# A residual in bf16, GELUs in batches and another key order in a two-layer attention and mixer kernel

## The chip, the cores and the metric

The kernel runs on one core of one Trainium2 chip. The time is the device time of one execution in microseconds (us), as the median of several executions; there is one core, so the slowest core is that core. Five engines of the core appear in this text. PE multiplies matrices, ACT (ScalarE) computes exponentials, GELUs and scaled copies, DVE (VectorE) does elementwise work and statistics, POOL (GpSimd) does small work on the side, and SP only starts transfers here. Every run lists the mean clock that the throttle granted PE, as a share of full speed.

## The reference, cut to what matters

```python
B, S, D, H, F = 1, 2048, 448, 16, 1792          # Dh = 28

def _A_ref(x, wqkv, wo):                        # attention
    q, k, v = ...                               # x @ wqkv, 16 heads of 28
    scores = jnp.einsum("bhqd,bhkd->bhqk", q, k) * (Dh ** -0.5)
    p = _softmax(scores, axis=-1)
    return ... @ wo

def _B_ref(x, w1, w2, w3, w4):                  # mixer
    h = _gelu(_layernorm(x, axis=-1) @ w1)
    ...                                         # four quarters of h shifted along S, then @ w2
    x1 = x + hs
    h2 = _gelu(_layernorm(x1, axis=-1) @ w3) @ w4
    return x1 + h2

x = A_x                                         # everything is bf16
for _ in range(2):                              # written out in the original
    x = x + _A_ref(_layernorm(x), A_wqkv, A_wo)
    x = x + _B_ref(_layernorm(x), B_w1, B_w2, B_w3, B_w4)
```

The softmax needs 2 x 16 x 2048 x 2048 exponentials, about 134 million. GELU is needed on 2 x 2048 x (448 + 1792) elements. In the trace of the kernel before, a table load of 1.283 us stands wherever ACT changes from exponentials to its GELU function (9 times) or back (8 times). (Most of the 448-wide GELUs are built from a tanh, of which 32 stand in this trace, 28 with a mean of 642 ns and 4 with 410, none of them with a table load.)

## The kernel before: the parts that matter

The rows are cut into 16 tiles of 128. Four tiles make a unit of 512 queries (the last unit of layer 2 is halved). The program is written as many small generator tasks; a scheduler in the same file runs them against modelled durations, with a list of seeds (`MOVES`) that breaks its ties, and fixes one order of instructions for each engine before the kernel is built. The attention loop hands ACT one exponential after another. Each reads one to three PSUM banks of scores, and everything else has to fit around it.

```python
x_res = sb("x_res", [128, NT, D], FP32)          # the residual, 16 tiles
h2T   = sb("h2T", [128, 14, 512], BF16)          # w3's output, up to 4 tiles wide
...
# the exponential (t_attention)
yield op("act", e_dur(n), lambda e, ...: e.activation(out=PT[:, p0:p0 + cnt, :],
         in_=ps[:, b0:b0 + cnt, :], func=ACT.Exp, scale=SCALE), ..., tab="exp", main=n, ...)
...
# the second half of the mixer for up to four tiles (t_mixB)
yield from par(prio, [w3_group(fch) for fch in range(14)])   # PE -> PSUM -> DVE copy -> h2T
...
if not direct:
    yield op("act", c_act(14 * NW), lambda e: e.activation(out=h2T[:, :, hoff:hoff + NW],
             in_=h2T[:, :, hoff:hoff + NW], func=ACT.Gelu_apprx_tanh),
             reads=allk, writes=allk, tab="gelu", margin=1.0)     # one in-place GELU
...
yield from par(prio, [w4_tile(i, t) for i, t in enumerate(tiles)])
```

Nine such GELUs run, eight among the 821 exponentials and one right behind the last. In the trace each has a table load of 1.283 us ahead of it, and the eight have one behind them, ahead of the next exponential. The last three tiles of layer 2 use small GELUs that read PSUM directly ("direct"), after the exponentials.

The keys of a layer are worked through in parts, because a unit's queries can start before all keys exist. `ORDER` lists (unit, part) for the units that start that way:

```python
PARTS = {0: [(0, 4), (4, 8), (8, NT)], 1: [(0, 8), (8, 12), (12, NT)]}   # key tiles of a part
ORDER = {0: [(0, 0), (0, 1), (0, 2)], 1: [(0, 0), (1, 0), (0, 1), (1, 1), (0, 2), (1, 2)]}
```

Where the scheduler sees PE with too little work in the last 4 us, it inserts fillers: matmuls of ones into a free PSUM bank, whose result nobody reads. They are meant to keep PE's clock up; what taking 14 of them out of the head does is measured in e5_dip below (6.83 us at half clock).

```python
WIN, TARGET = 4.0, 0.8
def keep_pe_busy(self, until):
    ...
    while self.cur["pe"] + dur + 0.12 < until:
        used = ...                       # modelled busy time of PE in the last WIN us
        if used > self.TARGET * self.WIN:
            self.cur["pe"] = t + 0.1
            continue
        ...                              # pick a free bank
        self.P.add("pe", lambda e, b=pick: fn(e, b), reads, [key(pick)], t_end=t + dur)
```

## Time and profile before

The median is 1090.22 us of 3 runs (1089.98 to 1091.11). The profiled execution spans 1089.3 us.

| part of the span | us | how it is read |
|---|---|---|
| head, to the first exponential | 22.82 | timeline of ACT |
| first to last exponential | 1028.12 | windows; ACT busy 1014.31, idle 13.81 |
| tail, after the last exponential | 38.36 | windows |

The windows view of the kernel before gives that table. Its columns are the window, its length, then the busy time of PE, PEld (weight loads), DVE, ACT and POOL with the number of instructions, then the granted PE clock, the DMA share and GB/s. I cut the stretch of exponentials at 88.69 us, where ACT does a small scaling.

```profile
22.82:88.69 65.87, 62.33 (x487) 21.13 (x492) 58.48 (x160) 60.14 (x55) 6.17 (x8) 1.00 0.25 69
88.69:1050.94 962.25, 933.35 (x8519) 356.05 (x8529) 517.62 (x1139) 954.17 (x828) 41.66 (x49) 1.00 0.13 31
1050.94:1089.30 38.36, 34.03 (x332) 22.77 (x328) 18.73 (x48) 16.29 (x39) 5.03 (x7) 1.00 0.05 16
```

The reader is to see that ACT is idle 5.73 us in the first of these windows (65.87 - 60.14) and 8.08 us in the long one. PE looks just as busy, but its share contains fillers: 1225 of them in the whole program, 180.8 us. The bound is ACT: what takes work off ACT in the stretch shortens the run.

Where ACT's time goes is in its groups by shape (line, engine, operation, shapes, count, then busy us and the mean ns of one, then idle time before them), here those of the kernel before:

```profile
L1181 ACT ACTIVATE PT<-ps 128x1536 bf16<-128x1536 f32 x410 | 599.2, 1462 | 10.6 <-PE ps L1155 8.1
L1181 ACT ACTIVATE PT<-ps 128x1024 bf16<-128x1024 f32 x407 | 422.2, 1037 | 2.0 <-PE ps L1155 2.0
...
L1478 ACT ACT_TABLE_LOAD x9 | 11.5, 1283 | 0.2
L1181 ACT ACT_TABLE_LOAD x8 | 10.3, 1283 | 0.1
```

There are 18 table loads with the first one of the program: 9 for gelu, 8 back to exp. How one switch looks is in the timeline of ACT of the kernel before (start, duration, what):

```profile
600.17 1.28 ACT L1478 ACT_TABLE_LOAD   x1
601.46 3.19 ACT L1478 ACTIVATE h2T<-h2T 128x3584 bf16<-128x3584 bf16 x1
604.67 1.28 ACT L1181 ACT_TABLE_LOAD   x1
605.97 2.37 ACT L1181 ACTIVATE PT<-ps 128x1024 bf16<-128x1024 f32 x2
```

Each instruction starts where the one before it ended. A pair of loads costs 2 x 1.283 us here and nothing more that can be seen.

The start of the stretch, in the same view of the same kernel, has the longest single wait (in brackets: how long ACT was idle before, and what ended it):

```profile
22.82 7.14 ACT L1181 ACTIVATE PT<-ps 128x1536 bf16<-128x1536 f32 x6 [0.20 <-PE ps L1155]
34.90 29.52 ACT L1181 ACTIVATE PT<-ps 128x1536 bf16<-128x1536 f32 x26 [4.93 <-PE ps L1155]
```

### The profile page before, as it was taken

Reading aid. Unit: us, or ns where it says so; the run is one execution under the profiler, and the core shown is the slowest. Engines: PE = TensorE matmul, PEld = TensorE weight load, DVE = VectorE, ACT = ScalarE, POOL = GpSimd, SP = SyncE. Lnnn points to the kernel's source line nnn. Section 1 sums busy time; section 2 is a strip of 40 time slices with the busy share of each in tenths; the row PEclk is TensorE's granted clock in tenths of the full one; section 3 lists DMA queues with packets and bytes.
Section 4 is the critical chain, followed back from the end, with each engine's and each line's share of the span. In section 5 each row is a group of like instructions: output and inputs, shape, how many; then the busy total and the mean of one; then the engine's idle time right before and its main releaser. Section 6 shows DMA issues by size and latency. Waiting matters only on the chain.

```text
span 1089.3 us, 21738 instructions
## 1 busy us (share of the span) xinstructions
PE 1048.6 (96%) x9482; PEld 411.8 (38%) x9501; DVE 610.5 (56%) x1414; ACT 1044.3 (96%) x938; POOL 59.5 (5%) x80
## 2 busy tenths in 40 slices
PE   8999999999999999999999999999999999999998
PEld 4333333334333433333334333343333333434455
DVE  7985348411683358533787345525884646566453
ACT  6899999999999999999999999999999999999983
POOL 3100000000010000100001000000001000000010
PEclk9999999999999999999999999999999999999999
DMA  7222070000000000000011101222201000110000
GB/s 197 78 69 69 21 182 20 16 1 20 20 2 20 20 21 20 20 1 20 20 40 45 30 30 50 78 68 50 55 5 35 14 20 11 34 25 11 14 16 22
DMA packets 76968, 40.64 MB, mean 37 GB/s; under 512 B 61192, under 2 KB 70280, under 8 KB 76872
## 3 DMA queue, kind: packets, MB, share of 16 engines
q1 hardware_dynamic: 74760, 35.58, 13.0%
q0 software_dynamic: 2112, 3.67, 1.4%
q8 instruction: 74, 1.21, 0.5%
q14 instruction: 22, 0.18, 0.1%
HBM read 14.20 MB, written 8.13 MB: 21 GB/s over the span
## 4 chain that ended last, share of the span: by engine, by line
ACT 57%; PE 36%; DVE 5%; issue 1%; DMA 0%; SPq 0%; ACTq 0%; DVEq 0%
ACT PT L1181 50%; PE ps L639 10%; PE ps L1155 10%; PE ps L1205 8%; PE ps L642 4%; PE ps L1540 4%; ACT h2T L1478 4%; ACT gt L1297 1%; ACT L1478 1%; ACT L1181 1%; DMA h2T<-in_A_wqkv_dram 0%; DVE qT L909 0%; ACT h2T L1468 0%; DVE hT L1288 0%; DVE qT L944 0%
## 5 line engine op out<-in xcount | busy, mean ns | idle before, releaser
L1181 ACT ACTIVATE PT<-ps 128x1536 bf16<-128x1536 f32 (+1 forms) x821 | 938.8, 1247 | 12.6 <-PE ps L1155 10.1
L1155 PE MATMUL ps<-qT,kT 32*128 32x512 bf16 (+1 forms) x2304 | 319.4, 360 | 12.8 <-ACT PT L1181 7.1
L1205 PE MATMUL ps<-PT,vaug 128*32 128x512 bf16 (+1 forms) x2304 | 263.6, 362 | 3.0 <-ACT PT L1181 0.8
L1540 PE MATMUL ps<-ones_bf 128*128 128x256 bf16 x1225 | 180.8, 276 | 2.6 <-DVE hot L673 1.1
L1155 PEld LDWEIGHTS ps<-qT,kT 32*128 32x128 bf16 x2304 | 80.1, 91 | 260.7 <-ACT PT L1181 149.3
L1471 DVE CAST h2T<-ps 128x512 bf16<-128x512 f32 (+2 forms) x126 | 73.8, 586 | 126.1 <-PE ps L639 91.9
L1540 PEld LDWEIGHTS ps<-ones_bf 128*128 128x128 bf16 x1225 | 102.1, 98 | 81.2 <-issue 57.9
L639 PE MATMUL ps<-xT,w 112*128 112x512 bf16 (+6 forms) x581 | 118.1, 324 | 1.6 <-DVE h2T L1471 0.6
L1205 PEld LDWEIGHTS ps<-PT,vaug 128*32 128x32 bf16 x2304 | 67.6, 94 | 130.9 <-issue 76.3
L639 PE MATMUL ps<-w,h2T 128*128 128x448 bf16 x302 | 68.9, 354 | 5.3 <-ACT h2T L1478 5.0
L639 PEld LDWEIGHTS ps<-xT,w 112*128 112x128 bf16 (+1 forms) x581 | 45.7, 104 | 49.3 <-issue 26.0
L642 PE MATMUL ps<-xT,w 112*32 112x512 bf16 (+3 forms) x780 | 63.6, 340 | 0.3 <-DVE uin L1489 0.2
L1227 DVE SCALAR_TENSOR_TENSOR u_sb<-uin,fct,ps 128x512 f32<-128x512 f32 x24 | 17.8, 742 | 62.6 <-PE ps L1205 59.1
L642 PE MATMUL ps<-w,h2T 128*32 128x448 bf16 x584 | 46.4, 368 | 4.5 <-ACT h2T L1478 4.5
L1496 DVE TENSOR_TENSOR x_res<-x_res,ps 128x448 f32<-128x448 f32 x16 | 9.8, 619 | 71.2 <-PE ps L639 48.5
L1478 ACT ACTIVATE h2T<-h2T 128x7168 bf16<-128x7168 bf16 (+2 forms) x9 | 45.1, 5015 | 0.1
L1430 POOL TENSOR_TENSOR mst<-mst,neghalf 128x1 f32<-128x1 f32 x32 | 23.8, 747 | 297.7 <-DVE mst L1428 297.7
L639 PEld LDWEIGHTS ps<-w,h2T 128*128 128x128 bf16 x302 | 25.0, 97 | 35.1 <-issue 11.7
L909 DVE TENSOR_SCALAR qT<-ps,bcol 128x512 bf16<-128x512 f32 (+1 forms) x24 | 15.3, 653 | 40.7 <-PE ps L639 39.3
L802 DVE BATCH_NORM_STATS2 st<-x_res 128x6 f32<-128x448 f32 x60 | 36.9, 615 | 0.7
L1332 POOL TENSOR_TENSOR mst<-mst,neghalf 128x4 f32<-128x4 f32 (+2 forms) x10 | 9.1, 906 | 486.9 <-DVE mst L1331 273.7
L642 PEld LDWEIGHTS ps<-xT,w 112*32 112x32 bf16 (+1 forms) x780 | 24.0, 95 | 11.8 <-DVE hT L1288 0.6
(141 smaller groups left out, 908.0 us busy)
## 6 DMA issues: line engine op xcount, KB each, us to landing
uscr<-u_sb SPq DMA_DIRECT2D x24, 256.0 KB, 2.0
uin<-uscr SPq DMA_DIRECT2D x24, 256.0 KB, 2.8
x_res<-in_A_x_dram POOLq DMA_DIRECT2D x4, 896.0 KB, 7.4
w<-in_B_w_dram SPq DMA_DIRECT2D x2, 1568.0 KB, 13.8
out_dram<-uin SPq DMA_DIRECT2D x16, 112.0 KB, 1.7
h2T<-in_A_wqkv_dram SPq DMA_DIRECT2D x2, 392.0 KB, 5.6
w<-in_B_w_dram SPq DMA_DIRECT2D x2, 392.0 KB, 8.3
xT<-xn SPq DMA_TRANSPOSE x32, 3.7
```

The lines of the kernel that those rows point to most:

```text
L639: return e.matmul(out=dst(0, m), lhsT=lhs(0, m), rhs=rhs, start=start, stop=stop)
L642: return [e.matmul(out=dst(a, min(m, a + 32)), lhsT=lhs(a, min(m, a + 32)), rhs=rhs, start=start, stop=stop, tile_position=(0, a)) for a i ...
L802: yield op("dve", 0.55, lambda e: e.bn_stats(out=st6[:, t, :], in_=w4[:, t, :] if staged else x_res[:, t, :]), reads=[(("w4",), t // 2) if ...
L909: yield op("dve", 0.06 + c_ps(nw), lambda e, b=b: e.tensor_scalar(out=dst, in0=ps[:, bi(b), 0:nw], scalar1=bias, scalar2=None, op0=ALU.add ...
L1155: yield op("pe", 0.005 if ph == h else 0.012 + W / 2400.0, lambda e, bk=bk, r0=32 * j, g=g, kc=kc, q0=q0, W=W, c0=W * h: e.matmul(out=ps[: ...
L1181: yield op("act", e_dur(n), lambda e, b0=b0, p0=p0, cnt=cnt: e.activation(out=PT[:, p0:p0 + cnt, :], in_=ps[:, b0:b0 + cnt, :], func=ACT.E ...
L1205: yield op("pe", 0.004 + nt * 0.0133, lambda e, j=j, rhs=rhs, vs=vs, i=i: e.matmul(out=ps[32 * j:32 * j + 32, UBK, 0:128 * nt], lhsT=vaug[ ...
L1227: yield op("dve", 0.06 + c_ps(W), lambda e: e.scalar_tensor_tensor(out=u_sb[:, 0:W], in0=uin[:, :], scalar=fct[:, L, p, g:g + 1], in1=ps[: ...
L1430: yield op("pool", 0.57, lambda e, t=t: e.tensor_tensor(out=mst[:, t, R3:R3 + 1], in0=mst[:, t, V3E:V3E + 1], in1=neghalf[:, 0:1], op=ALU. ...
L1471: yield op("dve", c_ps(NW), lambda e, fch=fch, b=b: e.tensor_copy(out=h2T[:, fch, hoff:hoff + NW], in_=ps[:, bi(b), 0:NW]), reads=[("ps", ...
L1478: yield op("act", c_act(14 * NW), lambda e: e.activation(out=h2T[:, :, hoff:hoff + NW], in_=h2T[:, :, hoff:hoff + NW], func=ACT.Gelu_apprx ...
L1540: SC.fill = (0.13, lambda e, b: e.matmul(out=ps[:, bi(b), 0:256], lhsT=ones_bf[:, :], rhs=ones_bf[:, :].unsqueeze(1).to_broadcast([128, 2, ...
```

## The change

The intent has three parts. The residual is kept in bf16, as the reference rounds it anyway. The GELUs of neighbouring groups of tiles run one right after the other, so that a pair shares the two table loads; for that `h2T` becomes twice as wide. In layer 2, unit 0 gets all its keys before unit 1 gets its last two parts. Around these, the loads of x go to SP's queue without conversion, and the scheduler has new seeds. The diff, cut to its core:

```diff
-    ORDER = {..., 1: [(0, 0), (1, 0), (0, 1), (1, 1), (0, 2), (1, 2)]}
+    ORDER = {..., 1: [(0, 0), (1, 0), (0, 1), (0, 2), (1, 1), (1, 2)]}
-    TAILB = [[NT - 3], [NT - 2, NT - 1]]
+    MIXB = [      # (tiles, first slot of h2T, batch; None is direct), for each layer
+        [([0, 1, 2], 0, 0), ([3, 4, 5, 6], 4, 0), ([7, 8, 9, 10], 0, 1), ([11, 12], 4, 2), ([13, 14, 15], 0, 2)],
+        [([0, 1, 2], 4, 0), ([3, 4, 5, 6], 0, 0), ([7, 8, 9, 10], 4, 1), ([11, 12], 0, 1), ([13], 2, None), ([14, 15], 4, None)],
+    ]
-        x_res = sb("x_res", [128, NT, D], FP32)
+        x_res = sb("x_res", [128, NT, D], BF16)
-        h2T = sb("h2T", [128, 14, 512], BF16)
+        h2T = sb("h2T", [128, 14, 1024], BF16)
...      # x: chunk 0 straight to x_res (before: to a second place in bf16, which the first tiles read)
-            for c in (1, 2, 3, 0)[:NCH]:
-                yield op("pool", 0.8, ... e.dma_start(out=x_res[:, 4 * c:4 * c + 4, :], ...
+            for c in range(1, NCH):
+                yield op("sp", 0.1, ... e.dma_start(out=x_res[:, 4 * c:4 * c + 4, :], ...
...
-                yield op("act", c_act(14 * NW), ... func=ACT.Gelu_apprx_tanh), ..., tab="gelu", margin=1.0)
+                yield ("sig", ("w3", L, tiles[0]))
+                yield ("wait", ("gelu", L, tiles[0]))
...
+        def t_gelu(L, batch):
+            for (t, h0, n) in batch:
+                yield ("wait", ("w3", L, t))
+            for k, (t, h0, n) in enumerate(batch):
+                ...
+                yield op("act", c_act(14 * NW), ... func=ACT.Gelu_apprx_tanh),
+                         reads=allk, writes=allk, tab="gelu", margin=0.0 if k else 1.0, glue=k > 0)
+                yield ("sig", ("gelu", L, t))
...      # MOVES: new seeds; now a list of lists, with one attempt for each (there is one list)
```

The first two parts belong together. The bf16 residual frees 16 x 448 x 2 = 14336 bytes of a partition, and the wider `h2T` takes 14 x 512 x 2 = 14336. So the main worth of the bf16 residual is that it makes room for the batching.

## The prediction

> **What bounds it now.** ScalarE (ACT). By the windows view it is busy 1014.3 of the 1028.1 us between the first attention exponential (22.82 us, timeline) and the end of the last (1050.94). The groups show 821 exponentials, 938.8 us. PE's 96% is padded by 1225 filler matmuls (180.8 us); DVE has 576 us there. Outside lie a head of 22.8 us and a tail of 38.4 us, chains across engines. Of ACT's 13.8 us idle in the stretch, 4.93 us are one wait, before the seventh exponential, for PE's scores.
>
> **Batched GELUs.** Before, each of 9 in-place GELUs (3.19, 4.68 or 6.18 us) has its own table load, and 8 loads bring exp back: 18 loads with the first. The built order of the new kernel has 12. [...] the trace shows 1283 ns, and at 600.17 us exp to GELU to exp runs 1.28, 3.19, 1.28 us[...], so I count only the load, plus the 0.1 us by which neighbouring exponentials overlap (58 take 66.7 us, mean 1.247 alone). Six loads fewer: -8.3 us. Given back: the last 256-wide GELU stood after the last exponential and now stands before the last ten: +3.1 us. GELU work is the same otherwise.
>
> **Key order.** Layer 2's segments break groups of exponentials more often: 823, +0.2 us. Unit 0 finishes earlier, so mixer work spreads better; that saves part of about 5 us of small waits in 12 places: -1.5 us. Risk: layer 2 needs the third key chunk some 24 exponentials (28 us) after layer 1's last GELU batch, before about 53. I work out the chain from there (w4, residual, statistics, transposes, K projection) as about 17 us, so no stall above 2 us.
>
> **bf16 residual.** Normalizations reading x_res fall from 513 to about 400 ns (the group that reads bf16 already), 88 of them, 10 us of DVE. Statistics (613 against 615 ns by input type) and adds with a PSUM operand (618, 619) don't gain. [...] DVE is off the path outside head and tail: under 1 us. The converting loads and the second copy of chunk 0 go, but loads landed before DVE used them: nothing.
>
> **Head and tail.** All but one of the Q projections now stand before the first scores (16 matmuls more, about 4 us of PE, partly in gaps): first exponential 2 to 3 us later, the 4.93 us wait shorter; together +1. The tail stays a chain PE, DVE, POOL, ACT; leftover w4 matmuls (28 before, about 36 now, most ahead of the transposes, where fillers stood) and 4.5 us of load and GELU move off it: -1.5 us.
>
> **Sum.** -8.3 +3.1 +0.2 -1.5 +1 -1.5 = about -7 us: **1083.0 us**, 8 in 10 between 1076 and 1089. Chances: faster by over 2% 0.03, within 2% 0.96, slower 0.01.
>
> **Signs.** 12 table loads; ACT busy between first and last exponential about 1009 us; 823 exponentials at unchanged durations; normalizations near 400 ns; tail 36 to 38 us; first exponential at 25 to 26 us; the wait near the seventh under 4 us.
>
> **What would make it wrong.** ACT stalling for layer 2's third and fourth key chunks (after about 512 exponentials); small waits after the longer breaks (about 13 us of GELU in one piece), when w4 matmuls for seven tiles crowd PE; a tail that grows because leftover matmuls don't fit its gaps; a much better head.

The sum came to -8.3 +3.1 +0.2 -1.5 +1 -1.5 = -7.0 us. The -8.3 are six loads of 1.283 us and six times the 0.1 us of overlap, which the page before shows: 821 exponentials of 1.247 us are 1023.8 us one by one, and ACT is busy with them for 938.8 us, so each overlaps by 0.10 us.

## The result, and the profile after

| | runs | median us | range us | granted clock of the runs |
|---|---|---|---|---|
| before | 4 | 1090.66 | 1089.98 to 1091.36 | profiled one 0.998 |
| after | 4 | 1086.46 | 1085.44 to 1086.76 | 0.995, 0.995, 0.997, 0.995 |

The ratio is 0.996, with a 95% interval of 0.9943 to 0.9977: within 2%, and a little faster. A ratio in this text is the mean time of one kernel's fast runs over the mean of the other's in the same rounds, so it is not quite the ratio of the medians quoted beside it. The prediction of 1083.0 us was 3.5 us too low, and its range of 1076 to 1089 held.

The same windows for the kernel after, cut at the same small scaling, which is at 90.49 us here:

```profile
30.11:90.49 60.38, 57.54 (x429) 18.60 (x434) 50.95 (x141) 58.26 (x53) 2.10 (x2) 1.00 0.27 75
90.49:1048.12 957.63, 929.93 (x8449) 354.14 (x8457) 505.95 (x1138) 950.30 (x827) 40.97 (x49) 1.00 0.13 31
1048.12:1084.60 36.48, 32.91 (x348) 22.07 (x345) 18.85 (x48) 12.82 (x39) 3.99 (x7) 0.99 0.07 23
```

These lines and those of before add up to the whole difference. The span is ACT's busy time in the stretch, plus the head with the waits of the first window (start of the first exponential and ACT's idle time to the cut), plus the later waits, plus the tail:

| us | before | after | change | predicted |
|---|---|---|---|---|
| ACT busy, first to last exponential | 1014.31 | 1008.55 | -5.76 | -5.0 (-8.3 +3.1 +0.2) |
| head and first waits (22.82 + 5.73; 30.11 + 2.12) | 28.55 | 32.23 | +3.68 | +1 |
| later waits of ACT | 8.08 | 7.33 | -0.75 | -1.5 |
| tail | 38.36 | 36.48 | -1.88 | -1.5 |
| span | 1089.30 | 1084.59 | -4.71 | -7 |

The part that was meant to gain has gained. The groups of ACT by shape, kernel after:

```profile
L1183 ACT ACTIVATE PT<-ps 128x1536 bf16<-128x1536 f32 x410 | 599.8, 1463 | 3.9 <-PE ps L1157 2.3 <-PE ps L1207 0.3
L1183 ACT ACTIVATE PT<-ps 128x1024 bf16<-128x1024 f32 x405 | 420.9, 1039 | 3.8 <-PE ps L1157 2.9 <-PE ps L1207 0.8
...
L1511 ACT ACT_TABLE_LOAD x5 | 6.4, 1283 | 0.1
L1183 ACT ACT_TABLE_LOAD x5 | 6.4, 1283 | 0.1
...
L1352 ACT ACT_TABLE_LOAD x1 | 1.3, 1283 | 0.0
```

With the first load of the program that is 12 loads instead of 18, and the exponentials last as long as before. One batch in the timeline of ACT, kernel after, shows two GELUs (of 4.68 and 6.17 us) between one pair of loads:

```profile
352.05 1.28 ACT L1511 ACT_TABLE_LOAD   x1
353.34 10.75 ACT L1511 ACTIVATE h2T<-h2T 128x5376 bf16<-128x5376 bf16 x2
364.11 1.28 ACT L1183 ACT_TABLE_LOAD   x1
```

The start of the stretch, in the same view, has moved by 7.29 us, where 2 to 3 us had been expected:

```profile
30.11 2.37 ACT L1183 ACTIVATE PT<-ps 128x1536 bf16<-128x1536 f32 x2
32.82 3.78 ACT L1183 ACTIVATE PT<-ps 128x1536 bf16<-128x1536 f32 x3 [0.35 <-PE ps L1157]
37.78 7.80 ACT L1183 ACTIVATE PT<-ps 128x1024 bf16<-128x1024 f32 x7 [1.18 <-PE ps L1157]
```

The wait of 4.93 us has become one of 1.18 us, which pays for half of the delay. Where much of the rest went shows in two views of the head. First the windows of the kernel before, then those of the kernel after; the clock is the third number from the end:

```profile
15.00:18.00 3.00, 1.86 (x23) 1.06 (x23) 2.24 (x8) 0.77 (x2) 0.00 (x0) 1.00 1.56 381
18.00:21.00 3.00, 3.00 (x15) 0.95 (x13) 3.00 (x12) 2.00 (x3) 0.00 (x0) 1.00 0.85 201
```

```profile
12.00:15.00 3.00, 1.62 (x21) 1.10 (x22) 1.46 (x3) 1.76 (x3) 0.00 (x0) 1.00 0.20 69
15.00:18.00 3.00, 1.84 (x26) 1.16 (x25) 2.18 (x11) 0.69 (x1) 0.55 (x1) 0.63 0.03 8
18.00:21.00 3.00, 2.55 (x10) 0.87 (x8) 1.51 (x9) 0.60 (x1) 0.86 (x1) 0.50 0.00 0
```

Before, PE's clock is full through the head. After, it is half from 15.76 to 22.59 us by the trace's record of the clock. That lasts 6.83 us. Second, the timeline of PE, kernel before and then kernel after:

```profile
14.51 1.02 PE L639 MATMUL ps<-xT,wq_pad 112*128 112x512 bf16 x4
...
17.45 2.02 PE L639 MATMUL ps<-xT,wk_pad 112*128 112x512 bf16 x8
```

```profile
9.65 2.14 PE L1547 MATMUL ps<-ones_bf 128*128 128x256 bf16 x18
13.29 0.43 PE L852 MATMUL ps<-ident,xn 128*112 128x128 bf16 x4 [1.50 <-ACT xn L894]
...
16.94 1.91 PE L643 MATMUL ps<-xT,wq_pad 112*128 112x512 bf16 x4 [1.16 <-DVE sc L761]
...
20.41 2.97 PE L643 MATMUL ps<-xT,wk_pad 112*128 112x512 bf16 x8
```

The same four matmuls take 1.91 us instead of 1.02, and the same eight 2.97 instead of 2.02. Ahead of it PE ran dry: the scheduler put 18 fillers (line L1547) before a wait for ACT that lasted 1.50 us, and then came small transposes and matmuls with one column.

A similar thing happens near the end, in both of these profiled runs. After the last long GELUs the fillers stop too early, PE is idle until the GELU ends (2.21 us before, 2.29 us after), and for 3.41 us of the w4 matmuls behind it the clock is at 0.50 (from 1014.3 us before, from 1032.9 us after). The timeline of PE, before and then after:

```profile
1006.89 4.43 PE L1540 MATMUL ps<-ones_bf 128*128 128x256 bf16 x39
1013.53 4.51 PE L642 MATMUL ps<-w,h2T 128*32 128x448 bf16 x56 [2.21 <-ACT h2T L1478]
```

```profile
1025.36 4.54 PE L1547 MATMUL ps<-ones_bf 128*128 128x256 bf16 x40
1032.19 7.17 PE L643 MATMUL ps<-w,h2T 128*128 128x448 bf16 x28 [2.29 <-ACT h2T L1511]
```

Up to the end of the program the falls in the traces last 3.41, 6.83 or 10.24 us, which is one, two or three times 3.41 us, and the clock in them is 0.50. Their length varies between runs of one kernel (6.83 us in the head of this profile of the kernel after, 10.24 us in that of e0_after). In the three batches of experiments below, the kernel before ran 29 times. In 10 of those the mean clock is 1.0 and the mean time 1090.03 us; in 19 it is 0.998 and the mean time 1091.36 us. The kernel after ran 9 times in all, never with a full clock, with a mean of 1086.56 us.

The bf16 residual, finally, shows in the groups of DVE. Kernel before, then kernel after:

```profile
L871 DVE TENSOR_SCALAR xn<-x_res,mv,rstd 128x448 bf16<-128x448 f32 x56 | 25.7, 513 | 1.1 <-POOL rstd L1004 1.1
...
L1404 DVE TENSOR_SCALAR x1b<-x_res,mv,mst 128x448 f32<-128x448 f32 x32 | 15.6, 506 | 0.1
```

```profile
L873 DVE TENSOR_SCALAR xn<-x_res,mv,rstd 128x448 bf16<-128x448 bf16 x56 | 19.6, 402 | 3.3 <-POOL rstd L1006 3.3
...
L1406 DVE TENSOR_SCALAR x1b<-x_res,mv,mst 128x448 f32<-128x448 bf16 x32 | 15.3, 506 | 0.1
```

The normalization with a bf16 output falls from 513 to 402 ns when its input is bf16 too. In the one with an fp32 output nothing changes (506 and 506).

### The profile page after: what moved, and what is told of

It is laid out like the page before. It is cut to its first block, busy times and chain, and to the rows that moved or that the text cites. A ratio compares the mean times of both kernels' runs of the same rounds, so it can differ in the third digit from the quotient of the medians.

```text
span 1084.6 us, 21565 instructions
## 1 busy us (share of the span) xinstructions
PE 1046.1 (96%) x9390; PEld 409.4 (38%) x9408; DVE 597.5 (55%) x1410; ACT 1036.5 (96%) x938; POOL 54.1 (5%) x76
## 4 chain that ended last, share of the span: by engine, by line
ACT 60%; PE 34%; DVE 5%; DMA 1%; issue 0%; SPq 0%; DVEq 0%; ACTq 0%
ACT PT L1183 53%; PE ps L643 12%; PE ps L1157 8%; PE ps L1207 7%; ACT h2T L1511 4%; PE ps L646 4%; PE ps L1547 2%; ACT gt L1299 1%; DMA h2T<-in_A_wqkv_dram 1%; ACT L1511 1%; ACT L1183 0%; DVE kT L911 0%; DVE st L805 0%; DVE hT L1290 0%; DVE xn L873 0%
## 5 line engine op out<-in xcount | busy, mean ns | idle before, releaser
L1183 ACT ACTIVATE PT<-ps 128x1536 bf16<-128x1536 f32 (+1 forms) x823 | 938.3, 1246 | 7.7 <-PE ps L1157 5.2
L1207 PE MATMUL ps<-PT,vaug 128*32 128x512 bf16 (+1 forms) x2304 | 249.8, 362 | 3.3 <-ACT PT L1183 1.4
L1547 PE MATMUL ps<-ones_bf 128*128 128x256 bf16 x1234 | 185.1, 277 | 2.5 <-DVE hot L677 1.1
L1547 PEld LDWEIGHTS ps<-ones_bf 128*128 128x128 bf16 x1234 | 102.4, 98 | 85.5 <-issue 62.8
L643 PE MATMUL ps<-xT,w 112*128 112x512 bf16 (+6 forms) x632 | 127.8, 323 | 0.8 <-ACT h2T L1470 0.4
L643 PEld LDWEIGHTS ps<-xT,w 112*128 112x128 bf16 (+1 forms) x632 | 50.5, 104 | 52.6 <-issue 29.6
L643 PE MATMUL ps<-w,h2T 128*128 128x448 bf16 x259 | 62.2, 362 | 4.0 <-ACT h2T L1511 4.0
L646 PE MATMUL ps<-xT,w 112*32 112x512 bf16 (+3 forms) x576 | 48.8, 349 | 0.1
L1490 DVE TENSOR_TENSOR uin<-x_res,ps 128x448 bf16<-128x448 bf16 x16 | 9.8, 619 | 66.1 <-PE ps L643 49.8
L1497 DVE TENSOR_TENSOR x_res<-x_res,ps 128x448 bf16<-128x448 bf16 x16 | 9.9, 621 | 64.3 <-PE ps L646 35.3
L805 DVE BATCH_NORM_STATS2 st<-x_res 128x6 f32<-128x448 bf16 x64 | 39.1, 615 | 2.1 <-DMA x_res<-in_A_x_dram 1.3
L1223 DVE STREAM_TRANSPOSE u_sb<-ps 128x512 f32<-128x512 f32 (+1 forms) x24 | 15.0, 625 | 34.5 <-PE ps L1207 34.5
```

Of the source, the lines that this page charges most:

```text
L643: return e.matmul(out=dst(0, m), lhsT=lhs(0, m), rhs=rhs, start=start, stop=stop)
L646: return [e.matmul(out=dst(a, min(m, a + 32)), lhsT=lhs(a, min(m, a + 32)), rhs=rhs, start=start, stop=stop, tile_position=(0, a)) for a i ...
L805: yield op("dve", 0.55, lambda e: e.bn_stats(out=st6[:, t, :], in_=x_res[:, t, :]), reads=[("x", t)], writes=[("st6", t)])
L1183: yield op("act", e_dur(n), lambda e, b0=b0, p0=p0, cnt=cnt: e.activation(out=PT[:, p0:p0 + cnt, :], in_=ps[:, b0:b0 + cnt, :], func=ACT.E ...
L1207: yield op("pe", 0.004 + nt * 0.0133, lambda e, j=j, rhs=rhs, vs=vs, i=i: e.matmul(out=ps[32 * j:32 * j + 32, UBK, 0:128 * nt], lhsT=vaug[ ...
L1547: SC.fill = (0.13, lambda e, b: e.matmul(out=ps[:, bi(b), 0:256], lhsT=ones_bf[:, :], rhs=ones_bf[:, :].unsqueeze(1).to_broadcast([128, 2, ...
```

## The experiments

The theory is that the missing 3 us were lost to PE's clock: the new head leaves PE with too little work between 12 and 18 us (busy 1.62 and 1.84 of 3.00 us in the windows above), the clock halves, and the head is late by about 2 us. The late fall adds to it. The rivals are these. The x loads moved to SP's queue, beside the loads of the weights, so perhaps they delay ACT's preparation of the weights, and the low clock is only a bystander. Or the head is late because more Q projections stand before the first scores, whatever the clock. Or the batching gives part of its saving back.

There are twelve runs in three batches, each batch on one chip: the first four kernels on one (before there: 1090.88 us median, 11 runs), b1_late, e5_dip, e8_dense and e6_unbatch on a second (before: 1091.12 us, 9 runs), and the last four on a third (before: 1091.26 us, 9 runs). All results were correct. Most edits act on the finished order of instructions, just before it is emitted. `P.ops["pe"]` is PE's list, and this helper adds n fillers behind its instruction i:

```python
def more_fill(i, n, bank=None):
    pe, at = P.ops["pe"], P.ops["pe"][i]
    fn = at.fn if bank is None else lambda e: SC.fill[1](e, bank)
    extra = [_Op("pe", fn, False) for _ in range(n)]
    ...                                   # same position in the global list
    pe[i + 1:i + 1] = extra
```

### e0_after: the changed kernel again

No edit. What was expected:

> The changed kernel again, as the yardstick for the other runs on this chip. About 0.996 of before, 1086.5 us; granted clock 0.995; in the head the clock at half from about 15.8 to 22.6 us, first exponential near 30.1 us.

Measured: 1086.88 us (1086.06 to 1087.46, 5 runs), ratio 0.9963 (0.995 to 0.9976), the clock 0.995 in all five. The profiled run had the clock at half for 10.24 us in the head, and its first exponential came at 31.74 us. The result repeats in this batch, and the fall of the clock in the head with it. The fall was 3.41 us longer than expected, and the first exponential came 1.6 us later than expected.

### e1_fill: fillers where PE ran dry

```diff
+        more_fill(78, 12)            # 18 fillers become 30, up to the transposes at 13.3 us
```

> The changed kernel with 12 more filler matmuls just before PE's idle stretch that ends at 13.3 us. Theory (the head is late because this idle stretch lets the TensorE clock fall to half from 15.8 to 22.6 us): the clock stays 1.0 there, the first exponential starts at 27 to 28 us instead of 30.1, and the run is 1.5 to 2.5 us shorter than e0_after. Rivals (the early loads of x, or the order with more Q projections in front): the first exponential moves by less than 0.3 us, and so does the time.

Measured: 1085.95 us (1084.6 to 1087.71, 5 runs), ratio 0.9956 (0.9944 to 0.9968). The clocks are 0.998, 1.0, 0.998, 0.995 and 0.995. The profiled run (1084.66 us) had no fall in the head, and its first exponential came at 27.92 us, 2.19 us earlier than in the kernel after; the late fall was there. The timeline of PE of this kernel shows the filled gap and the four matmuls at their full speed again:

```profile
9.42 3.45 PE L1547 MATMUL ps<-ones_bf 128*128 128x256 bf16 x30
13.27 0.43 PE L852 MATMUL ps<-ident,xn 128*112 128x128 bf16 x4 [0.39 <-ACT xn L894]
...
16.75 1.03 PE L643 MATMUL ps<-xT,wq_pad 112*128 112x512 bf16 x4 [0.99 <-DVE csum L746]
```

Twelve matmuls that compute nothing made the head faster in this run, which speaks for the theory. But two of the five runs have a mean clock as low as the kernel after, so this one gap isn't the whole condition. The time alone, with its overlapping intervals, would not have told e1_fill from e0_after.

### e2_xlate: the x loads held back

```diff
+        for x in P.ops["sp"][5:8]:                       # x chunks 1 to 3
+            x.deps[P.ops["sp"][3].ekey] = P.ops["sp"][3] # wait for the Q weights
```

> The changed kernel with the three loads of x (chunks 1 to 3) held back on SP until the Q weights have landed, as they were in before, where they stood behind POOL's work. Rival R1 (these loads take bandwidth from the weights): the Q weights land near 6.9 us instead of 8.9, the last of the first transposes comes at 12.5 instead of 13.3, and 0.8 us is gained; if the shorter idle stretch also keeps the clock up, 2 to 3 us. Clock theory alone: the clock still falls and at most 0.8 us is gained. Order theory: nothing.

Measured: 1086.16 us (1082.71 to 1087.7, 6 runs), ratio 0.9954 (0.9942 to 0.9966). The issue of these loads moved from 3.39 to 8.96 us, yet ACT's wait for the Q weights ended at 8.97 us, where it had ended at 8.88 in the kernel after and at 9.32 in e0_after. The profiled run had a fall of 10.24 us in the head, as long as that of e0_after, and the first exponential at 31.52 us. So the transfers were not what held ACT up, and this rival falls. One of its six runs had a clock of 1.0, and that run took 1082.71 us; the other five had 0.994 to 0.997 and took 1085.92 to 1087.7. In these six runs of one kernel on one chip, the time follows the clock.

### e3_both: the two together, with fewer fillers

```diff
+        ...                          # the dependency of e2_xlate
+        more_fill(78, 8)
```

> Both edits, with 8 fillers. If clock and loads are both causes: 2.5 to 3.5 us shorter than e0_after, first exponential at 26 to 27.5 us. What then remains against 22.8 us in before is the order, about 4 us of matmuls and evictions of the Q and V projections that now stand in front.

Measured: 1086.19 us (1084.51 to 1087.0, 5 runs), ratio 0.9955 (0.9944 to 0.9967), clocks 0.995, 0.998, 0.998, 0.997, 0.998. The profiled run still had a fall of 6.83 us in the head and its first exponential at 29.79 us. This was a miss: eight fillers did not hold the clock in the profiled run, and the experiment tells nothing about a sum of two effects. PE's wait before the transposes had shrunk to 0.56 us here and the clock fell, while in the profile of e1_fill it was 0.39 us and the clock stayed; two profiles show no threshold.

### e5_dip: the opposite edit, on the kernel before

If thin work on PE is the cause, taking fillers out of the head of the kernel before has to bring the fall there, with its loads and its order of Q projections unchanged.

```diff
+        for a, b in ((88, 92), (69, 79)):                # 14 fillers
+            gone = P.ops["pe"][a:b]
+            P.ops["pe"][a:b] = []
```

> The kernel before with 14 fillers of its head taken out (around 10 to 13 us), so that PE idles there as it does in the changed kernel. Clock theory: in most runs the clock falls to half in the head, mean clock 0.995 to 0.997, first exponential at 25 us instead of 22.8, 2 to 3 us longer than before. Rival (idle PE in the head costs nothing): no change, these fillers compute nothing that is used.

Measured: 1092.52 us (1091.85 to 1095.74, 5 runs), ratio 1.002 (1.0007 to 1.0032), clocks 0.997, 0.996, 0.995, 0.992, 0.997. The windows of this kernel:

```profile
12.00:15.00 3.00, 1.48 (x11) 0.96 (x12) 1.95 (x7) 2.59 (x4) 0.00 (x0) 0.50 1.55 389
15.00:18.00 3.00, 3.00 (x17) 1.15 (x16) 0.81 (x5) 0.69 (x1) 0.58 (x1) 0.50 1.55 381
```

The clock is half for 6.83 us, the four Q matmuls take 1.87 us instead of 1.02, and the first exponential comes at 25.37 us instead of 22.82. PE had less to do and finished later. Not all of the 2.55 us are the clock's: ACT's first normalization already started at 8.15 us instead of 7.34, ahead of the fall at 11.57 us. From that normalization to the first exponential it takes 17.22 us here and 15.47 to 15.49 us in all four profiles of this order without a fall in the head (before, e4_bf16only, b1_late, b2_late). So about 1.7 us are the clock's. That settles it for this head: with 14 fillers less the clock fell to half for 6.83 us, and that delayed the first exponential by about 1.7 us.

### b1_late: a failed edit

This was meant to fill the late gap of the kernel before. The search for the place was wrong, and the 18 fillers went into a busy place, where a run of 4 fillers became one of 22.

```diff
+        more_fill(ends[-2], 18)      # not the gap it was meant for
```

> The kernel before with 18 more fillers in its own last GELU break, where its clock falls in about half of its runs. Clock theory: all runs at clock 1.0 and 1089.9 to 1090.2 us, as its own runs at clock 1.0; no more than 1 us better than before. With e8_dense this compares the two kernels with neither losing the clock: about 7 us apart, as predicted.

Measured: 1092.55 us (1091.85 to 1093.67, 5 runs), ratio 1.0015 (1.0002 to 1.0027), with clocks of 0.998, 1.0, 1.0, 0.998, 0.998. It says nothing about filling the late gap. It does show where else a fall can lie: in its profiled run (0.998) the only fall of 3.41 us before the end of the program comes behind an earlier GELU, at 494.77 us, where PE had idled 2.03 us. In the profile of the kernel before, the same break with the same 2.03 us brought no fall. So a mean clock of 0.998 doesn't say that the late fall came. The run also shows that fillers aren't free: with a clock of 1.0 its two runs average 1091.89 us against 1090.02 for three of the kernel before in this batch, so 18 fillers in a busy place cost 1.9 us.

### b2_late: the late gap of the kernel before, in the right place

```diff
+        more_fill(ends[-1], 18)      # 39 fillers become 57, up to the end of the last long GELU
```

> What b1_late meant to be (there the 18 fillers went into a wrong, busy place): the kernel before with 18 more fillers in its last GELU break, 39 become 57. Clock theory: every run at clock 1.0 and 1089.9 to 1090.3 us, as its own runs at clock 1.0; about 1 us under its runs at 0.998.

Measured: 1090.27 us (1090.05 to 1091.28, 5 runs), ratio 0.9993 (0.9981 to 1.0006), clocks 1.0, 1.0, 0.998, 1.0, 0.998. In the profile, PE's idle time before the w4 matmuls fell from 2.21 to 0.24 us, and 56 of them took 2.83 us instead of 4.51. That every run would have a full clock was a miss: two of five have 0.998 (19 of 29 for the kernel before), too few runs to say that falls became rarer, and where these two lie isn't known. With a full clock this kernel is no faster than before with a full clock (1090.05 to 1090.27 against 1090.16 and 1089.96). By the windows view, ACT's later waits are 7.13 us in this profile, which has no fall, and 8.08 us in that of the kernel before, which has the late one. So the late fall is worth about 1 us in a run that has it.

### e7_late: the late gap of the kernel after, alone

```diff
+        more_fill(max(i for i, x in enumerate(P.ops["pe"]) if x.oid is None), 18)
```

> The changed kernel with the 18 late fillers alone, the head as it was. The late fall of the clock goes, that of the head stays: mean clock 0.995 to 0.997, about 1 us better than the changed kernel's runs with both falls, 1085 to 1086.5 us; e8_dense's other 2.5 to 3 us are the head's.

Measured: 1086.59 us (1085.49 to 1087.59, 5 runs), ratio 0.9955 (0.9941 to 0.9968), clocks 0.995, 0.997, 0.997, 0.997, 0.995. The profiled run has no late fall (28 w4 matmuls take 5.48 us instead of 7.17), and the fall in the head is there at 10.24 us, with the first exponential at 31.27 us. So the two falls are separate, and the one in the head doesn't go with the late one. The gain of about 1 us that was expected doesn't show in the time: the median is just above the range that was named, and the interval of the ratio overlaps that of e0_after.

### e8_dense: fillers in both places

```diff
+        more_fill(max(i for i, x in enumerate(P.ops["pe"]) if x.oid is None), 18)
+        more_fill(171, 5, "b5")
+        more_fill(126, 4)
+        more_fill(119, 8, "b5")
+        more_fill(78, 12)
```

> The changed kernel with filler matmuls in four gaps of the head (12, 8, 4 and 5) and 18 more after the last long GELU break. Clock theory: every run has a mean granted clock of 1.0 and takes 1082 to 1083.5 us, as the one run of e2_xlate at clock 1.0 did (1082.71), against 1086.9 for e0_after. If the clock is not what costs the time: 1086 or more, with the clock at 1.0.

Measured: 1083.19 us (1082.85 to 1083.61, 5 runs), ratio 0.9928 (0.9915 to 0.9942), and the clock is 1.0 in all five. Five of the 29 fillers meant for the head stand just behind the first exponential. The windows of this kernel, cut as before:

```profile
27.87:88.44 60.57, 59.52 (x440) 18.92 (x439) 51.04 (x141) 58.26 (x52) 2.10 (x2) 1.00 0.26 75
88.44:1045.02 956.58, 932.85 (x8478) 355.43 (x8475) 505.65 (x1138) 950.08 (x827) 40.97 (x49) 1.00 0.13 31
1045.02:1081.50 36.48, 32.91 (x348) 22.09 (x345) 18.84 (x48) 12.82 (x39) 3.99 (x7) 1.00 0.07 24
```

The span is 3.10 us shorter than in the kernel after. The head and first waits are 27.87 + 2.31 = 30.18 us, 2.05 less than there; the later waits are 6.50 us, 0.83 less; ACT's busy time is 0.22 less; the tail is the same. Against the three runs of the kernel before with a full clock in this batch (mean 1090.02 us), e8_dense is 6.8 us faster. That is what the change is worth when the clock is the same on both sides, and it is close to the 7 us that were predicted.

The profiles of all runs that share the order of the kernel after agree on the head. Counted from the transposes that stand at 13.29 us in the kernel after, the first exponential comes 14.61 and 14.65 us later without a fall there (e8_dense, e1_fill), 16.82 to 16.84 us later with one of 6.83 us (after, e3_both, e6_unbatch), and 18.00 to 18.14 us later with one of 10.24 us (e0_after, e2_xlate, e7_late). The head is still 1.63 us later than before (30.18 against 28.55), so the rival of the order of Q projections isn't excluded for that remainder.

### e6_unbatch: the batching undone

A one-column exponential between the two GELUs of each of the four pairs forces both loads back, with everything else of the kernel after in place.

```diff
+        for x, y in zip(list(act), list(act)[1:]):
+            if x in gelus and y in gelus:
+                z = _Op("act", lambda e: e.activation(out=spare[:, :], in_=ones_f[:, 0:1], func=ACT.Exp), False)
+                act.insert(act.index(x) + 1, z)
```

> The changed kernel with a one-column exponential between the two GELUs of each of the four batches of two, so that each GELU has its own pair of table loads again. If a pair costs what the trace shows, two loads of 1.283 us and about 0.2 us for the small exponential, and ACT sets the time there: 4 x 2.8 = 11 us longer than e0_after. [...] If the batches are off the path: under 4 us.

Measured: 1100.78 us (1100.12 to 1102.35, 4 runs), ratio 1.0092 (1.0078 to 1.0105), clocks 0.989 to 0.991. Its timeline of ACT:

```profile
357.71 1.28 ACT L1587 ACT_TABLE_LOAD   x1
359.00 0.20 ACT L1587 ACTIVATE spare<-ones_f 128x1 f32<-128x1 f32 x1
359.21 1.28 ACT L1512 ACT_TABLE_LOAD   x1
```

Eight loads and four exponentials of 0.203 us are 11.1 us by their durations. ACT's busy time between the first and last exponential rose by 12.1 us (1020.68 against 1008.55), and the time by 13.9 us against e0_after (by their medians, from two batches). Every load here takes 1283 ns. The durations leave a rest of 13.9 - 11.1 = 2.8 us. Of this rest, ACT's waits in the stretch rose by 2.1 us (11.55 against 9.46), together with four or five more falls of the clock of 3.41 us each behind the longer breaks (mean clock 0.989 in this profile, 0.995 in that of the kernel after); I take them for the cause, but no run separates it. So the batching does not give its saving back.

### e4_bf16only: the residual alone

```diff
-        x_res = sb("x_res", [128, NT, D], FP32)
+        x_res = sb("x_res", [128, NT, D], BF16)          # in the kernel before
```

> The kernel before with its residual in bf16 and nothing else, the order of instructions the same on every engine. Predicted: normalizations at about 400 ns instead of 513, statistics and adds unchanged, under 1 us of the whole, most of it in the tail. If the time of DVE set the pace: 5 us or more. Compare runs of equal clock (before: about 1090.0 at 1.0, 1091.2 at 0.998).

Measured: 1089.37 us (1089.33 to 1090.93, 5 runs), ratio 0.9988 (0.9975 to 1.0). Every engine has the order of instructions of the kernel before. With a full clock, three of its runs average 1089.35 us against 1090.06 for two of the kernel before, so the bf16 residual alone gains 0.7 us. DVE's busy time falls from 610.5 to 601.9 us in the profile, and the long wait of ACT at the start from 4.93 to 4.52 us. The group of the normalizations in this kernel:

```profile
L871 DVE TENSOR_SCALAR xn<-x_res,mv,rstd 128x448 bf16<-128x448 bf16 x56 | 19.2, 397 | 1.1 <-POOL rstd L1004 1.1
```

Against the 513 ns of the kernel before that is 116 ns less for each. The adds with a PSUM operand gain nothing: 618 and 619 ns before, 618 and 620 in this kernel.

### e9_order: the best version

e8_dense, with a hand-made order of the first 15 us: ACT prepares the weights of the first K projection and the second normalization sooner, DVE copies the fourth transposed tile before it squares, and PE starts the first K projection before the column sums.

```diff
+        put_before("act", (8, 2, 5, 9), 3)
+        put_before("dve", cp[3:4], sqs[0])
+        put_before("pe", (79, 80, 81, 82), 61)
+        put_before("pe", (95, 96, 97, 99), 83)
+        ...                          # dependencies computed anew
+        ...                          # fillers as in e8_dense, the 12 after the first K projection
```

> e8_dense with a hand-made order in the first 15 us: ACT normalizes its second tile before it waits for the Q weights and casts them, and the first squares, last transposes and first K projection follow it. Order theory (a part of the later head comes from what the schedule put in front): the first K projection's result is on ACT at 13.6 us instead of 15.3, the first exponential 1 to 1.7 us earlier than in e8_dense, 1081.5 to 1082.2 us. If the head is bound elsewhere (DVE): no gain.

Measured: 1082.68 us (1082.23 to 1083.19, 4 runs), ratio 0.9922 (0.9908 to 0.9935), the clock 1.0 in all four. The first K projection left PSUM at 13.28 us instead of 15.27, but the first exponential came only at 27.29 us instead of 27.87. Of a gain of 2 us at one step, 0.6 us arrived at the end. The expected range of 1081.5 to 1082.2 us was missed. This kernel has the lowest median, below both the kernel before and the kernel after, but the interval of its ratio overlaps that of e8_dense.

## Why the prediction was right or wrong, point by point

- **The table loads (-8.3, +3.1, +0.2).** This was right: 12 loads, exponentials of unchanged length (mean 1246 ns against 1247), ACT busy 1008.55 us where about 1009 was named. The sum of -5.0 was measured as -5.76. Most of the difference is that the 823 exponentials took 0.5 us less in all (938.3 against 938.8 us), not 0.2 us more. Counting only the load was right: in e6_unbatch, eight loads and four small exponentials came to 11.1 us by their durations, of the 13.9 us by which the run grew.
- **Key order and small waits (-1.5).** This came out at about half: the later waits fell by 0.75 us, and by 0.63 us with a full clock on both sides (6.50 us in e8_dense against 7.13 in b2_late). No stall over 2 us came for the third key chunk: ACT's waits there were 0.40, 0.42 and 0.16 us. The key order was not tested by itself, because the scheduler's seeds are tuned to it, and a run of it alone would also have measured a worse schedule. Its own share stays open.
- **The bf16 residual (under 1).** Right: 402 and 392 ns for the two kinds of normalization, and 0.7 us in e4_bf16only.
- **The tail (-1.5).** Right: it measured -1.88, a tail of 36.48 us.
- **Head (+1): this is the term that was mis-sized.** The prediction had the first exponential at 25 to 26 us and "together +1". It came at 30.11 us, and the head with its first waits measured +3.68 us. Of that, 2.05 us go when the clock stays full (e8_dense), so they are PE's clock, which the prediction had not asked about. It took the head's durations from the trace of before, where the clock is full, and never compared how densely PE is fed in the new order. The order of instructions could have shown it: the 18 fillers that stand before the second normalization take 2.14 us, and PE still waits 1.50 us behind them (30 fillers and 0.39 us in e1_fill). The other 1.63 us stand against the +1 of the prediction, and its two parts were further off than their sum: with a full clock the first exponential came at 27.87 us, about 2 us later than named, and the first waits shrank by 3.42 us, more than named. More Q projections stand before the first scores, as predicted; that they are the reason wasn't tested alone, and e9_order shows only that the K projection isn't what binds.
- **The sum.** -5.76 +3.68 -0.75 -1.88 = -4.71 us of the profiled spans, against -7. In runs with a full clock on both sides, the change is worth 6.8 us. The predicted size came out where the assumption behind it, an unchanged clock, held, but partly by luck. Between the profiles with a full clock, b2_late for the kernel before and e8_dense for the kernel after, the same four terms are -5.95 +1.51 -0.63 -1.83 = -6.90 us: table loads and tail gave 1.3 us more than predicted, waits and head 1.4 us less.

What also stays open is which work counts for the clock. Transposes and one-column matmuls stand in the thin stretch, and no run tested them alone. How long a gap or how little work brings a fall isn't shown either. In the head of the kernel after, 1.50 us of idle time and thin work behind it (PE busy 1.62 of 3.00 us between 12 and 15 us) were followed by a fall, and so were 2.21 us in the last GELU break of the kernel before, in its profiled run. An earlier break, with 2.03 us of idle PE each time, was followed by one in b1_late and by none in the profile of the kernel before. In the head, 8 fillers more did not hold the clock in the profiled run of e3_both, and 12 held it in that of e1_fill; 24 in three places of the head, with 5 just behind it and 18 in the late gap, held it in all 5 runs of e8_dense, and as many again in all 4 of e9_order. Outside the profiled runs only a run's mean clock is known, so where its falls lie isn't shown.

## What to carry to other kernels

When a change reorders the start of a kernel, or makes a break on another engine longer, look at how densely PE is fed there before trusting matmul durations from the old trace: here a stretch in which PE was busy for 1.62 of 3.00 us was followed by 6.83 us at half clock, and the four Q matmuls under that clock took 1.91 us instead of 1.02. Write the span as busy time of the bounding engine, plus head, plus waits, plus tail, and predict each, so that a wrong term can be found by subtraction. Compare runs with the same granted clock, because within one kernel the falls come and go, and they can hide a gain as large as the one you look for: of the six runs of e2_xlate, the one with a clock of 1.0 took 1082.71 us and the others 1085.92 to 1087.7, a spread of 3.2 to 5.0 us beside a measured gain of about 4 us.
